# Attention and FFN block on one core: the whole score stack loaded at a unit's start, four weight sums on VectorE, residual stores and one activation load at other places of SyncE's queue

## The chip, the cores and the metric

The kernel runs on one core of a Trainium2 chip. The metric is the device time of one execution in microseconds (us); a lower time is better. The five engines are TensorE (PE, with its weight loads shown as PEld), VectorE (DVE), ScalarE (ACT), GpSimd (POOL) and SyncE (SP). Each works through its own list of instructions in order, and semaphores hold an instruction until what it needs is done. SyncE computes nothing here: it issues DMA transfers. ScalarE issues some transfers too, between its computations, and an issue that has to wait holds the ScalarE instructions behind it.

## The reference

One transformer block on x of 2048 tokens by 576, all in float32. `silu(c) @ w_mod` gives six vectors: shift, scale and gate for attention (sa, ca, ga) and for the FFN (sb, cb, gb).

```python
h = _layernorm(x) * (1 + ca) + sa
x = x + ga * _A_ref(h, wq, wk, wv, wo, beta)
h = _layernorm(x) * (1 + cb) + sb
x = x + gb * ((_silu(h @ w_gate) * (h @ w_up)) @ w_down)
```

`_A_ref` has 32 heads of 18 columns and works on four segments of 512 tokens. Inside a segment it is a softmax attention with a mask of -1e9; to it, weighted by a gate per head, comes a memory read-out `phi(q) M / (phi(q) z)`, where M and z are sums over the segments before. The FFN is 576 to 4608 and back.

## The kernel before

**Number format.** Float32 values are split into a high and a low part (tiles ending in h and l, or "hi" and "lo" rows), and a product is made of three matmuls: high by high, high by low, low by high. The high part is a ScalarE or GpSimd copy, the low part a VectorE subtraction.

**Stages.** First (0 to 255 us) the projections to q, k and v of the four segments, written to DRAM in a layout for attention (kD, qD, vD). Then attention in 32 units of four heads of one segment, with the output projection and layer norm of earlier segments interleaved (255 to 618). Then the output projection of the last segment (618 to 643), together with the preparation of the FFN's first operands. Then the FFN (643 to the end), for two halves t of 1024 tokens and 18 pairs p of 256 hidden columns. The order of all instructions after the projections is written out by hand (a manual schedule): the program's order is the order on each engine.

**A unit of attention.** Unit u works on a "stack" of k rows (`kst`, 108 rows by 2 by 512) and q rows (`qst`, 110 rows by 4 by 512). The 108 rows are two halves e=0 and e=1 of 54; each half is one DMA for k and one for q (L164, L165; 216 KB each). There are four buffers, and `load_unit(u + 3, e)` in unit u fills the one that unit u-1 has used. A unit has eleven steps k. At each step three things advance: `p2_step` (L588 on), which makes the transposed scores of unit u with TensorE (L599) and their exponentials with ScalarE (L602); `p1_seq`, which makes the scores of unit u+2 (L182) and takes row maxima with VectorE (L187); and the events that the table PAT names. The maxima are transposed, copied by ScalarE (L205, event "n", at step 4 or 2) and written by two small DMAs (L170, 8 KB each) into rows 108 and 109 of `qst`, where matmul L599 of the next unit subtracts them. SyncE's order in a unit is: half e=0 at step 0, the two maxima rows at step 4 (or 2), half e=1 at step 5, then v (L664, in units that load the next segment's v), besides loads of qf, wo, x and stores placed by events.

**The output projection of segment 3** (L1401 to L1425): for each of four token tiles i and two halves h there are 14 matmuls (`wo_m`, L729) into one of two PSUM banks, and VectorE adds the bank to the residual x (`wo_x`, L734, "xr"). The next but one half needs that bank back. In between stand, by the lists SS, HH and WW, eight sums of FFN weight blocks (`sum_o`, L1157, four for each of the two O tiles of the first pair, z=0 and z=1), splits of FFN activations (`y_here`) and splits of FFN weights (`prep_w`, L1166 and L1167). ScalarE stores the finished residual tiles 0 to 2 (L1410), each in the middle of the next tile, and SyncE the last one (L1426).

**The FFN** makes each 2 by 2 block product with seven products m instead of eight, from sums of weight blocks (tile O, seven slots) and sums of activation blocks (tile y, seven operands o). The activation operands 0, 1, 5 and 3 of the first token half are loaded by SyncE (`load_y`, L1122 and L1123, 1024 and 192 KB each), the others are made on the core. The first pair multiplies in the order m = 1, 6, 2, 7, 5, 4; product 5 is the first that reads operand 3. At its start SyncE loads the first rows of w_down (`load_d`, L1174), ScalarE stores the weight sums for the second token half (L1141), and SyncE loads the next pair's weights (L1135) after those stores have landed, as there are two O tiles.

Of the kernel before, what the change touches and what calls it, by code (L numbers as in the profile page):

```python
# [67 lines left out]
def f32(ap):  # L68
    return ap.bitcast(F32)
# [3 lines left out]
def block(ctx: ExitStack, tc: tile.TileContext, x, wqk, wv, wo, beta, wgu, wd, c, w_mod, out):  # L73
    nc = tc.nc
    def pool(stk, name, bufs=1, **kw):
        return stk.enter_context(tc.tile_pool(name=name, bufs=bufs, reuse_waits="tile", **kw))
# [5 lines left out]
    def chain(*g):  # L82
        for a in g:
            yield from a

    def run(g):
        for _ in g:
            pass
# [26 lines left out]
    NB = 4  # L115
# [29 lines left out]
    xD = [dr.tile([P, 4, D], F32, tag=f"xD{s}", name=f"xD{s}") for s in range(NSEG)]  # L145
# [9 lines left out]
    NU = len(units)  # L155
    mcol, pmt, mrow = {}, {}, {}

    def load_stack(u, b, es=(0, 1)):
        s, q = units[u]
        for e in es:  # L160
            v = [d[s].rearrange("f z t -> (f z) t").rearrange("(Q a e r) t -> Q e r a t", Q=8, a=2, e=2)[q, e]
                 for d in (kD, qD)]
            r = slice(54 * e, 54 * e + 54)
            nc.sync.dma_start(f32(kst[b][r]), v[0])  # L164
            nc.sync.dma_start(f32(qst[b][r, e:4:2, :]), v[1])  # L165
# [408 lines left out]
    opl_ = pool(p2, "op2")  # L574
    ps = pool(p2, "ps2", 2, space=PSUM)

    def load_unit(u, e):
        if u < NU:
            load_stack(u, u % NB, (e,))

    def p1_seq(u):
        if NE <= u < NU:
            for i in range(4):
                yield from p1_step(u, u % NB, 3 - i, ps, wk, 4)
# [3 lines left out]
    def p2_step(u, j):  # L588
        if u >= NU:
            return  # L590
        n = L - 128 * j
        per = L // n if n <= 256 else 1
        pt = pp_.tile([P, 4, n], F32, tag=f"P{j}", name="Pt", bufs=1)
        Pt[u, j] = pt
        for h in range(0, 4, per):
            bank = ps.tile([P, L], F32, tag="s2", name="s2", bufs=S2B)
            for g in range(h, h + per, 2):
                w = min(per, 2)
                nc.tensor.matmul(bank[:, n * (g - h):n * (g - h + w)].rearrange("p (a b) -> p a b", a=w),  # L599
                                 lhsT=kst[u % NB][0:110, g // 2, 128 * j:128 * j + 128],  # L600
                                 rhs=qst[u % NB][0:110, g:g + w, 128 * j:L], start=True, stop=True)
            nc.scalar.activation(pt[:, h:h + per, :n], bank[:, :n * per].rearrange("p (a b) -> p a b", a=per),  # L602
                                 AF.Exp, scale=SCALE)
            if h + per < 4:
                yield
        nc.gpsimd.affine_select(out=pt[:, :, :P], in_=pt[:, :, :P], pattern=[[0, 4], [1, P]], compare_op=ALU.is_ge,
                                fill=0.0, base=0, channel_multiplier=-1)
        yield
# [52 lines left out]
    def load_v(s, j):  # L661
        if j == 0:
            vq[s] = vp.tile([P, 4, VC], F32, tag="vq", name=f"vq{s}")
        nc.sync.dma_start(vq[s][:, j, :], vD[s][:, j, :])  # L664
# [5 lines left out]
    op = pool(p2r, "op", side="right")  # L670
# [22 lines left out]
    def load_xr(s, i):  # L693
        xr = o3.tile([P, D], F32, tag="xr", name="xr") if s < 3 or i in (0, 3) else xp.tile([P, D], F32, tag="xs", name="xr")
        r = L * s + P * i
        nc.sync.dma_start(xr, x[r:r + P, :])
        return xr
# [10 lines left out]
    def wo_s(s, i):  # L708
        nc.scalar.copy(oT[s, i][0], pto[s, i])

    def wo_t(s, i):
        oh, ol, _ = oT[s, i]
        nc.vector.tensor_tensor(ol, pto.pop((s, i)), f32(oh), op=ALU.subtract)
# [17 lines left out]
    def wo_x(s, i, h):  # L731
        xr = oT[s, i][2]
        sl = slice(288 * h, 288 * h + 288)
        nc.vector.tensor_tensor(xr[:, sl], wps[0][:, :288], xr[:, sl], op=ALU.add)  # L734
        if h == 1 and s < 3:
            (nc.scalar if (s, i) == (2, 3) else nc.sync).dma_start(xD[s][:, i, :], xr)

    lnv = {}
# [235 lines left out]
    def stage_a():  # L974
        sc = flat(yh12[:, 1])
        xb = [sc[:, L * i:L * i + L].rearrange("p (a b) -> p a b", b=P) for i in range(2)]
        mb = mbd[:, 0:2].rearrange("p a b c -> p (a b c)")
        st = [v.rearrange("p (a b) -> p a b", b=256).bitcast(F32R) for v in (sc[:, 2 * L:3 * L], mb[:, :L], mb[:, L:2 * L], gaB[:, :L])]
        pts = {}
        for i in range(6):  # L980
            kb, kh = divmod(i, 2)
            u = 18 + i
            n = P if kb < 2 else 96
            h = yh(kh, kb)
            at(11 * (u - 1) + 1 if i else 11 * u, lambda i=i, kh=kh, kb=kb: load_cols(xb[i % 2], 0, 0, kh, kb))
            g = step_of(u) if i else 11 * u + 10
            at(g, lambda i=i, n=n: trans4(xb[i % 2], n, pts, i))
            at(g + 1, lambda i=i, h=h, kh=kh, kb=kb: scaled(h, flat(pts.pop(i)), kh, kb))
            for hv in range(2):
                y_part(g + 2 + 3 * hv, kh, kb, h[:, 256 * hv:256 * hv + 256], lambda j=2 * i + hv: st[j % 4], hv)  # L990
# [130 lines left out]
    def load_y(t, o):  # L1121
        nc.sync.dma_start(f32(y[:, o, 0:4]), yD[t][o][:, 0:4])  # L1122
        nc.sync.dma_start(f32(y[0:96, o, 4]), yD[t][o][0:96, 4])  # L1123
# [4 lines left out]
    def flush():  # L1128
        while later:
            later.pop(0)()  # L1130
# [20 lines left out]
        nc.scalar.copy(r[0:96, c], o[0:96, c, 2, :])  # L1151
        later.append(lambda: nc.vector.tensor_tensor(r[32:64, c], o[32:64, c, 2, :], f32(r[32:64, c]), op=ALU.subtract))

    def sum_o(p, z, j):
        o = O[p, z]
        d, a, b, op = ((4, 3, 2, ALU.add), (5, 4, 0, ALU.subtract), (3, 0, 3, ALU.subtract), (6, 1, 5, ALU.subtract))[j]
        nc.gpsimd.tensor_tensor(o[:, d], o[:, a], o[:, b], op=op)  # L1157

    def store_r(p, z):
        nc.scalar.dma_start(rD[p][z], f32(R[z][0:96]))  # L1160
# [9 lines left out]
    def load_d(t, p):  # L1170
        RW[p] = r = rp.tile([P, 7, 288], F32, tag="d", name="dr_")
        if t == 0:
            for f in range(2):
                nc.sync.dma_start(r[:, 2 * f:2 * f + 2].rearrange("p a b -> p (a b)"), wd[2 * p + f])  # L1174
        else:
            nc.sync.dma_start(r[:, :NS[p]], wdD[p][:, :NS[p]])
# [165 lines left out]
    with tc.manual_schedule():  # L1342
# [4 lines left out]
        event("f", -1)  # L1347
        for u in range(NU + 1):
            s, q = divmod(u, 8)
            load_unit(u + 3, 0)  # L1350
            ga = chain(*[p2_step(u, j) for j in range(4)])
            gb = p1_seq(u + 2)
            for k in range(11):
                next(ga, None)
                next(gb, None)
                if u == 17 and k == 0:
                    stage_a()
                if u == 24 and k == 0:
                    stage_b()
                for ev in PAT[q // 4 * 2 + u % 2][k].split():  # L1360
                    event(ev, u)
                for f in sched.pop(11 * u + k, ()):
                    f()
                if k == 5:
                    load_unit(u + 3, 1)
                    if 3 <= q < 7 and s < 3:
                        load_v(s + 1, q - 3)
            run(ga)
            run(gb)
        p2.close()  # L1370
# [9 lines left out]
        xr3 = {i: load_xr(3, i) for i in range(3)}  # L1380
# [7 lines left out]
        load_y(0, 1)  # L1388
        xr3[3] = load_xr(3, 3)
        load_y(0, 5)  # L1390
        load_y(0, 3)
        wo_r(3, 0)
        wo_z(3)
        wo_r(3, 1)
# [6 lines left out]
        for i in range(4):  # L1401
            for h in range(2):
                for c in range(WC):
                    n = 8 * i + 4 * h + c
                    wo_m(3, i, h, c, 2)
                    if c == 3:
                        wo_x(3, i, h)
                    flush()
                    if i > 0 and h == 0 and c == 1:
                        nc.scalar.dma_start(xD[3][:, i - 1, :], xr3[i - 1])  # L1410
                    if n in SS:
                        j = SS.index(n)
                        sum_o(0, j // 4, j % 4)
                    if n in HH:
                        y_here(HH.index(n))
                    if n in WW:
                        j = WW.index(n)
                        if j < 2:
                            prep_r(0, 0, 0, j)
                        prep_w(0, 0, next(gw))  # L1420
                if h == 1 and i < 2:
                    wo_r(3, i + 2)
                    wo_s(3, i + 2)
                    wo_t(3, i + 2)
        flush()  # L1425
        nc.sync.dma_start(xD[3][:, 3, :], xr3[3])  # L1426
        p2r.close()
        p5.close()
        accp = pool(p4, "acc")
# [4 lines left out]
        p6 = ExitStack()  # L1434
        new_acc(accp, (2, 3, 4, 5))
        load_d(0, 0)
        seq = [(p, z, m) for t in range(2) for p in range(NPR) for z in range(2) for m in MP]
        late = {}
        prev = None
# [6 lines left out]
        for t in range(2):  # L1446
            for p in range(NPR):
# [16 lines left out]
                for k in range(14):  # L1464
                    z, m = ZM[k]
# [93 lines left out]
                    if is_plain(t, p):  # L1559
                        if k in DK[dl // 2]:  # L1560
                            j = DK[dl // 2].index(k)
# [74 lines left out]
```

## Time and profile before

| what | us |
|---|---|
| median of 3 executions | 1909.57 |
| lowest and highest | 1909.08, 1915.14 |
| the profiled execution, its own time | 1911.3 |
| its span on the core | 1909.4 |
| TensorE busy in the span | 1872.0 |
| VectorE, ScalarE, GpSimd busy | 1507.0, 933.7, 584.5 |

The profile is of one execution. A line of it gives an engine, a source line (L599), the tile written and those read, and the time; "[0.63 <-DMA qs<-qD]" behind a line means that the engine stood idle for 0.63 us before this instruction, and that the last thing which released it was that transfer. An engine with a q (SPq, ACTq) issues a DMA: the duration is that of the issue, not of the transfer. In views by stretch of time the last two columns are the mean busy share of the core's 16 DMA engines and the rate at which they moved data. TensorE's granted clock was 1.00 in all the stretches shown, 0.93 in the first 50 us.

### The profile page before, as it was taken

To read this page: it belongs to the slowest core of one execution; us is meant where nothing else is said; L and a number is where in the kernel's file an instruction comes from. 1 tells how busy PE (TensorE), PEld (TensorE's weight loads), DVE (VectorE), ACT (ScalarE), POOL (GpSimd) and SP (SyncE) were. 2 spreads that over 40 slices of the span, in tenths; PEclk is the share of its full clock that TensorE was granted. 3 is DMA by queue.
4 is the path that set the end of the run, shared out by engine and by line. 5 is a ranking of instruction groups with operands and counts; after the bars stand their busy time and mean duration, and the time that the engine had idled before them with its cause. 6 is when DMAs were issued, how large, how long until landed. Compare 5 with 4: busy or idle time off the path is not lost.

```text
span 1909.4 us, 30712 instructions
## 1 busy us (share of the span) xinstructions
PE 1872.0 (98%) x10927; PEld 1560.4 (82%) x10927; DVE 1507.0 (79%) x3273; ACT 933.7 (49%) x2060; POOL 584.5 (31%) x787
## 2 busy tenths in 40 slices
PE   7999999999999899999999999999999999999999
PEld 4888866676766788888888888888888888888888
DVE  6566358878886888888888888866888888888887
ACT  1222267768767543454454454444445454454542
POOL 5212236555556645435445435400000000000000
PEclk9999999999999999999999999999999999999999
DMA  6767555445654854454454554477333333333331
GB/s 199 258 220 255 197 177 152 132 138 155 195 157 129 311 199 154 161 196 143 162 192 141 183 164 129 153 263 231 102 124 102 95 105 101 123 102 101 108 105 59
DMA packets 179424, 304.31 MB, mean 159 GB/s; under 512 B 26152, under 2 KB 107688, under 8 KB 177352
## 3 DMA queue, kind: packets, MB, share of 16 engines
q1 hardware_dynamic: 150264, 244.40, 40.9%
q10 hardware_dynamic: 29008, 57.96, 8.6%
q8 instruction: 86, 1.41, 0.3%
q14 instruction: 66, 0.54, 0.1%
HBM read 187.98 MB, written 113.77 MB: 158 GB/s over the span
## 4 chain that ended last, share of the span: by engine, by line
PE 88%; DMA 3%; DVE 3%; ACT 2%; POOL 1%; issue 1%; SPq 1%; ACTq 0%; DVEq 0%; POOLq 0%
PE A L1202 23%; PE pd L1323 13%; PE C L1202 11%; PE pd L1306 9%; PE B L1202 6%; PE pp L99 5%; PE s L599 4%; PE av L619 3%; PE s L182 3%; PE pv L99 3%; PE pw L729 2%; DMA qs<-qD 1%; DMA y<-yD 1%; PE pn L800 1%; ACT Pt L602 1%
## 5 line engine op out<-in xcount | busy, mean ns | idle before, releaser
L1202 PE MATMUL A<-y,wh 128*128 128x512 f32 x1152 | 406.1, 393 | 3.4 <-ACT B L1248 1.0
L187 DVE CUSTOM_DVE_ANT_0 junk<-s,tri 128x256 bf16<-128x256 f32 (+3 forms) x512 | 228.8, 487 | 71.9 <-PE s L182 64.4
L1167 DVE TENSOR_TENSOR wl<-O,wh 128x256 fp32r<-128x256 f32 x504 | 260.3, 521 | 2.8 <-ACT wh L1166 2.3
L1202 PEld LDWEIGHTS A<-y,wh 128*128 128x128 f32 x1152 | 216.6, 188 | 47.6 <-ACT B L1248 1.5
L1202 PE MATMUL A<-y,wl 128*128 128x512 f32 x576 | 226.7, 394 | 0.0
L602 ACT ACTIVATE Pt<-s 128x512 f32<-128x512 f32 (+1 forms) x352 | 188.0, 559 | 75.2 <-PE s L599 70.9
L1157 POOL TENSOR_TENSOR O<-O 128x384 f32<-128x384 f32 x144 | 164.6, 1156 | 169.2 <-DMA O<-in_wgu_dram 65.0
L1311 DVE TENSOR_TENSOR acc<-acc,pd 128x576 f32<-128x576 f32 x216 | 162.4, 752 | 58.6 <-PE pd L1306 52.0
L1202 PE MATMUL C<-y,wh 128*128 128x512 f32 x576 | 202.6, 392 | 1.6 <-DVE cu L1225 1.6
L1166 ACT CAST wh<-O 128x256 fp32r<-128x256 f32 x504 | 196.9, 405 | 7.6 <-DVE wl L1167 3.5
L1323 PE MATMUL pd<-dh,al 128*128 128x288 f32 x640 | 189.1, 296 | 0.0
L1323 PE MATMUL pd<-dh,ah 128*128 128x288 f32 x640 | 189.1, 295 | 0.0
L1323 PE MATMUL pd<-dl,ah 128*128 128x288 f32 x640 | 188.9, 295 | 0.0
L1327 DVE TENSOR_TENSOR acc<-acc,pd 128x576 f32<-128x576 f32 x156 | 116.9, 750 | 90.4 <-PE pd L1323 90.0
L1266 ACT CAST ah<-sg 128x512 fp32r<-128x512 f32 x192 | 119.2, 621 | 84.0 <-DVE sg L1226 77.9
L599 PE MATMUL s<-qs,ks 110*128 110x512 f32 (+2 forms) x384 | 150.1, 407 | 2.1 <-ACT Pt L602 2.0
L182 PE MATMUL s<-ks,qs 108*128 108x256 f32 (+3 forms) x512 | 141.1, 328 | 5.9 <-DVE mx L187 3.6
L1267 DVE TENSOR_TENSOR al<-sg,ah 128x512 fp32r<-128x512 f32 x192 | 135.8, 707 | 8.8 <-ACT ah L1266 8.5
L1306 PE MATMUL pd<-dh,ah 128*128 128x288 f32 x448 | 133.0, 297 | 0.0
L1306 PE MATMUL pd<-dh,al 128*128 128x288 f32 x448 | 132.5, 296 | 0.0
L1306 PE MATMUL pd<-dl,ah 128*128 128x288 f32 x448 | 132.3, 295 | 0.0
L1202 PEld LDWEIGHTS C<-y,wh 128*128 128x128 f32 x576 | 108.3, 188 | 22.2 <-DVE cu L1225 2.1
(360 smaller groups left out, 4405.4 us busy)
## 6 DMA issues: line engine op xcount, KB each, us to landing
O<-in_wgu_dram SPq DMA_DIRECT2D x36, 768.0 KB
oD<-O ACTq DMA_DIRECT2D x36, 512.0 KB
O<-oD SPq DMA_DIRECT2D x36, 512.0 KB
ks<-kD SPq DMA_DIRECT2D x64, 216.0 KB
qs<-qD SPq DMA_DIRECT2D x64, 216.0 KB
O<-in_wgu_dram SPq DMA_DIRECT2D x36, 384.0 KB
rD<-wr ACTq DMA_DIRECT2D x36, 336.0 KB
wr<-rD SPq DMA_DIRECT2D x35, 336.0 KB
```

Source lines behind the costliest of these rows:

```text
L99: nc.tensor.matmul(ps, lhsT=a, rhs=b, start=(k == 0), stop=(k == 13))
L182: nc.tensor.matmul(bank[:, n * (h - h0):n * (h - h0) + n], lhsT=qst[b][0:108, h, 128 * i:128 * i + 128], rhs=kst[b][0:108, h // 2, 0:n], s ...
L187: nc.vector.tensor_tensor_reduce(junk[:, :n], bank[:, n * (h - h0):n * (h - h0) + n], tri[:, L - n:], 1.0, -3e38, op0=ALU.add, op1=ALU.max ...
L599: nc.tensor.matmul(bank[:, n * (g - h):n * (g - h + w)].rearrange("p (a b) -> p a b", a=w), lhsT=kst[u % NB][0:110, g // 2, 128 * j:128 * ...
L602: nc.scalar.activation(pt[:, h:h + per, :n], bank[:, :n * per].rearrange("p (a b) -> p a b", a=per), AF.Exp, scale=SCALE)
L1157: nc.gpsimd.tensor_tensor(o[:, d], o[:, a], o[:, b], op=op)
L1166: nc.scalar.copy(wh, o)
L1167: later.append(lambda: nc.vector.tensor_tensor(wl, o, f32(wh), op=ALU.subtract))
L1202: nc.tensor.matmul(bank, lhsT=a, rhs=b, start=(first and n == 0), stop=(n == 6), skip_group_check=not first)
L1306: nc.tensor.matmul(pd[:, i, :288], lhsT=a[:, tk], rhs=w, start=(k == 0), stop=(k == 2))
L1311: nc.vector.tensor_tensor(o, o, pd[:, :, :288], op=ALU.add)
L1323: nc.tensor.matmul(pd[:, i, :288], lhsT=a[:, tk], rhs=w, start=(k == 0), stop=(k == 5))
```

## The change

Four things change; the computation stays the same.

- Both halves of a stack are loaded at step 0 of a unit. The maxima rows and v follow them on SyncE's queue.
- Of the eight weight sums in the last output projection, the four of z=1 are done by VectorE instead of GpSimd, at the same places of the written order.
- The residual tiles of segment 3 are all stored by SyncE, each right behind its last addition, as in the other segments.
- Operand 3 of the first half's activations is loaded behind the first w_down load, after the output projection, and no longer ahead of it.

```diff
-    def load_stack(u, b, es=(0, 1)):
+    def load_stack(u, b):
         s, q = units[u]
-        for e in es:
+        for e in range(2):
...
-    def load_unit(u, e):
+    def load_unit(u):
         if u < NU:
-            load_stack(u, u % NB, (e,))
+            load_stack(u, u % NB)
...
         nc.vector.tensor_tensor(xr[:, sl], wps[0][:, :288], xr[:, sl], op=ALU.add)
-        if h == 1 and s < 3:
+        if h == 1:
             (nc.scalar if (s, i) == (2, 3) else nc.sync).dma_start(xD[s][:, i, :], xr)
...
-    def sum_o(p, z, j):
+    def sum_o(p, z, j, eng=nc.gpsimd):
         o = O[p, z]
...
-        nc.gpsimd.tensor_tensor(o[:, d], o[:, a], o[:, b], op=op)
+        eng.tensor_tensor(o[:, d], o[:, a], o[:, b], op=op)
...
-            load_unit(u + 3, 0)
+            load_unit(u + 3)
...
-                if k == 5:
-                    load_unit(u + 3, 1)
-                    if 3 <= q < 7 and s < 3:
-                        load_v(s + 1, q - 3)
+                if k == 5 and 3 <= q < 7 and s < 3:
+                    load_v(s + 1, q - 3)
...
         load_y(0, 5)
-        load_y(0, 3)
...
                     flush()
-                    if i > 0 and h == 0 and c == 1:
-                        nc.scalar.dma_start(xD[3][:, i - 1, :], xr3[i - 1])
                     if n in SS:
                         j = SS.index(n)
-                        sum_o(0, j // 4, j % 4)
+                        sum_o(0, j // 4, j % 4, nc.vector if j > 3 else nc.gpsimd)
...
         flush()
-        nc.sync.dma_start(xD[3][:, 3, :], xr3[3])
...
         load_d(0, 0)
+        load_y(0, 3)
```

## The prediction

> **What bounds the kernel now.** I read the page's busy shares first, then the busy time by stage, then who waited for whom on TensorE, then the order in time around each wait.
>
> ```profile
> PE 1872.0 (98%) x10927; PEld 1560.4 (82%) x10927; DVE 1507.0 (79%) x3273; ACT 933.7 (49%) x2060; POOL 584.5 (31%) x787
> ```
>
> 98% is an average. By stage (attention, output projection of the last segment, start of the FFN, rest of the FFN; the columns are length, then busy PE, PEld, DVE, ACT, POOL, clock, DMA share, GB/s):
>
> ```profile
> 255.00:618.00 363.00, 355.09 (x2585) 237.81 (x2584) 290.19 (x1176) 270.55 (x556) 200.82 (x382) 1.00 0.52 149
> 618.00:643.00 25.00, 20.91 (x166) 19.70 (x159) 18.35 (x29) 10.02 (x21) 14.90 (x13) 1.00 0.93 335
> 643.00:675.00 32.00, 27.73 (x117) 21.15 (x116) 28.27 (x39) 18.43 (x42) 16.54 (x14) 1.00 0.81 274
> 675.00:1880.00 1205.00, 1203.97 (x6567) 1058.45 (x6566) 1015.16 (x1708) 568.95 (x1320) 276.67 (x251) 1.00 0.44 143
> ```
>
> From 675 on TensorE idles 1.0 us in 1205: nothing the diff touches can change that part, which only starts sooner or later. The diff edits the first three rows, where TensorE idles 7.9, 4.1 and 4.3 us. Two of its waits there belong to lines that the change moves (total, times, longest):
>
> ```profile
> PE pw L729 <- DVE xr L734: 3.4, 2, 1.8
> PE s L182 <- DMA qs<-qD: 2.2, 5, 1.0
> ```
>
> **Part 1, the stack load.** One unit in the order of time on SyncE's queue, the matmul that then waited, and the DMA share in between:
>
> ```profile
> 263.56 0.29 SPq L164 DMA_DIRECT2D ks<-kD  x1
> 263.89 0.35 SPq L165 DMA_DIRECT2D qs<-qD  x1
> 269.11 1.21 SPq L170 DMA_DIRECT2D qs<-mr  x2
> 270.36 0.49 SPq L164 DMA_DIRECT2D ks<-kD  x1
> 270.90 0.34 SPq L165 DMA_DIRECT2D qs<-qD  x1
> ...
> 275.72 0.47 PE L182 MATMUL s<-ks,qs 108*128 108x512 f32 x1 [0.63 <-DMA qs<-qD]
> ...
> 264.00:267.50 3.50, 3.50 (x32) 1.44 (x27) 2.45 (x13) 1.85 (x5) 3.08 (x6) 1.00 0.47 129
> 267.50:270.00 2.50, 2.33 (x13) 1.64 (x13) 2.25 (x9) 2.47 (x7) 0.64 (x1) 1.00 0.00 0
> ```
>
> The second half (e=1) stands behind the two maxima rows (L170), which wait for ScalarE's copy, and lands 4.8 us after its issue, at the first score matmul of the next unit. Issued at step 0 it goes out 6 us sooner, at about 264.3, and has the idle 267.5 to 270 to itself. All five waits (0.63, 0.17, 0.98, 0.15, 0.22) go: at most -2.15. The same loop of ScalarE and VectorE stands behind them (57 weight loads in this stage wait for the exponentials, 31.7 us), so some may come back as that wait; least gain 0. I take -2.0, since in each case PE was the engine that waited.
>
> What it adds: L170 now has 442 KB more ahead of it on SyncE's ring. A pair takes 3.2 us (264.3 to 267.45 in slices of half a microsecond). From the end of the second L170 issue to the next unit's first exponent-side matmul, which reads those rows, there are 3.85 us or more in every unit. Tightest is the one with L170 at 289.54: the first pair's data ends at 290.2 there, so the second would end by 293.4, and the rows are read at 294.54: 1.0 us spare; next 2.0. Cost 0; ends 0 and what rival C gives. v (L664), qf (L772) and wo (L904) keep their place after L170 or lose only the e=1 pair ahead of them; their users are a unit or more later.
>
> Whether the second pair really queues was bounded from 0 to 3.2 us, as the first pair fills only 0.58 to 0.63 of the 16 engines. [...]
>
> **Part 2, the output projection.** GpSimd's eight weight sums and VectorE at the same work with and without them:
>
> ```profile
> 625.89 10.38 POOL L1157 TENSOR_TENSOR O<-O 128x384 f32<-128x384 f32 x8
> ...
> 631.73 1.11 DVE L1167 TENSOR_TENSOR wl<-O,wh 128x256 fp32r<-128x256 f32 x1
> 637.10 0.41 DVE L1167 TENSOR_TENSOR wl<-O,wh 128x256 fp32r<-128x256 f32 x1
> ...
> 633.35 0.37 PE L729 MATMUL pw<-woh,oh 128*128 128x288 f32 x1 [1.55 <-DVE xr L734]
> 637.23 0.40 PE L729 MATMUL pw<-woh,oh 128*128 128x288 f32 x1 [1.80 <-DVE xr L734]
> ```
>
> While GpSimd sums, a VectorE instruction with both inputs in SBUF takes 1.1 to 1.5 us instead of 0.41 to 0.69. That backlog delays the residual add (xr), which frees the bank that TensorE waits for. With four sums left, GpSimd ends at 625.89 + 4 x 1.30 = 631.1. VectorE's rows from there at their short durations: wr ends 631.35, wl 631.8, xr 632.25 (was 633.21); wr 632.95, wl 633.35, y 634.1, xr 634.55 (was 637.18). TensorE's halves (1.9 us each) then start at 632.3, 634.6, 636.85, 638.75 and the last ends at 640.65, not 643.02: -2.4. The four sums on VectorE cost 0.55 each (between 0.41 for 256 and 0.68 for 512 columns), 2.2 us; one stands ahead of an add, three ahead of the last, at 639.75 to 641.4. No later half waits for the last add, and the first FFN bank doesn't either, so they cost TensorE 0; without that cover 1.2. Ends: -3.4 (both waits gone) and 0.
>
> The three residual stores leave ScalarE, which stood 3.50 and 2.51 us at them; it was not what TensorE waited for. On SyncE they wait for the adds in the order in which they come. Behind the last stand down's first load (L1174) and now y's operand 3: the last store would issue at 641.9 (was 643.71), L1174 at 642.4 and 642.8 (was 644.22), the y load at 643.3.
>
> **Part 3, the moved y load.** It was issued at 634.61, the small part at 642.68 (SyncE stood 7.7 us there, until a residual store had landed; now the store of the third tile, out by 639, is the one it waits for, and hides). It is read by the fifth product, at 650.45; with part 2 at about 648.05. What it now meets:
>
> ```profile
> 650.45 0.40 PE L1202 MATMUL C<-y,wh 128*128 128x512 f32 x1
> ...
> 616.00:640.00 24.00, 19.53 (x155) 17.24 (x155) 16.98 (x26) 9.87 (x20) 16.74 (x16) 1.00 0.99 350
> 640.00:644.00 4.00, 4.00 (x29) 3.82 (x29) 2.15 (x7) 1.24 (x3) 0.00 (x0) 1.00 0.44 154
> 644.00:650.00 6.00, 5.33 (x24) 4.02 (x23) 3.88 (x6) 4.39 (x10) 2.33 (x2) 1.00 0.96 312
> 650.00:659.00 9.00, 8.07 (x35) 6.33 (x34) 8.84 (x11) 5.91 (x13) 6.87 (x7) 1.00 0.93 316
> ```
>
> It leaves a stretch that ends idle (0.44) and joins one that is full until 659. Ahead of it on its queue are the last store (0.29 MB) and L1174 (0.59), beside it ScalarE's two weight stores (1.05 MB); itself it is 1.25 MB. From 642 at 310 to 350 GB/s it lands at 648.8 if ScalarE's queue gets nothing, 652.5 if the two share evenly. I take 650.9, between them: TensorE waits 2.8 us at the fifth product, which starts 0.45 later than before. Some comes back at once: the 0.93 us that the next product waited at 653.16 is for a copy behind VectorE, now ahead; from there it is 0.5 early. Then the second pair's weights: their first load (L1135, 649.98) waits for the weight store to land and stands behind y, so it gains nothing; the second was issued at 659.61, on VectorE's last weight split, about as early or late as TensorE. So the dense part starts 0.5 sooner. Ends: 2.9 sooner (y hidden), 2 later (even sharing and the weights behind it late by the rest of 1.25 MB / 0.34 = 3.7 us less 1.7).
>
> [...]
>
> **Sum.** -2.0 in attention and -0.5 at the start of the FFN: -2.5. The profiled execution took 1911.3 (span 1909.4 and 1.9 around it), so 1908.8; it is 1.7 above the median, 1909.57, against which the forecast is 1907.1.
>
> **Rivals.**
> A, the forecast: 1905.5 to 1908.5, 0.45.
> B, y lands in time and the gain of part 2 stays: -2.0 - 2.4 to -2.0 - 2.9, 1904.9; 0.22. For it: 640 to 644 is nearly idle. Against: 644 to 659 is full.
> C, slower: the maxima rows land behind the whole stack after they are needed. Price: beyond the spare, every microsecond of queueing costs one in each tight unit. It decides once a pair takes 1.1 us more than 3.2 in the tightest units; six units have 4.5 us or less after the issue; at 1 us each the forecast plus 6 is 1913.1, and at 1 us in half of the 28 units plus 14, 1921; above the time before from plus 2.5 on. For it: both pairs are alike and serial. Against: the 1.0 us is the worst case, and 3.85 us the least. 0.13.
> D, VectorE's slow rows don't come back or y lands after 653: no gain in part 2, +2 at the FFN: 1909.57 - 2.0 + 2 to + 4, 1909.6 to 1911.6; 0.20. For it: the sums are added to the engine that made TensorE wait.
>
> The time is that of A. The range reaches from B's better end to most of D and the start of C: 1903 to 1913. A measurement of this kernel can tell about 0.3% (5.7 us) from no change; Faster needs the far ends together (-2.15, -3.4 and some of the third row's 4.3 us of idle): 0.08, out of B. Slower is C's worse half, with 0.03 out of D: 0.1. Within: 0.82.
>
> **What would show it.** Right: no wait of L182's matmul for qs; the wl rows between 631 and 637 at 0.41; TensorE's first FFN product at about 640.7 less 2; then a wait of the fifth product for y of 2 to 3 us. Wrong: a wait of L599's matmuls for qs<-mr (C); no wait for y (B); the first add rows still late, or the stage from 675 on shorter or longer than 1234.

## The result, and the profile after

The changed kernel takes 1908.87 us (median of 20 runs, 1902.93 to 1915.08), the kernel before, beside it, 1913.87 (20 runs, 1909.08 to 1918.15). The ratio is 0.9977 with a 95% interval from 0.9969 to 0.9986: 4.4 us faster, between 2.7 and 5.9. That is a change of 0.2%, inside the 0.3% of the forecast, and more than its 2.5 us. Ratios here and below are of executions in the faster of two states, which leaves out one execution of e8 (3659.63 us).

All stages in the tables below are cut at the same instructions of TensorE: the first exponent-side matmul (L599) of unit 0, that of unit 31, the first FFN product (L1202), and the first matmul of the down projection. Each row is one profiled execution (us).

| | ahead of attention | attention | output projection | start of the FFN | rest | span |
|---|---|---|---|---|---|---|
| before | 254.96 | 354.10 | 33.96 | 34.67 | 1231.71 | 1909.4 |
| after | 256.81 | 349.68 | 31.42 | 37.65 | 1231.14 | 1906.7 |
| difference | +1.85 | -4.42 | -2.54 | +2.98 | -0.57 | -2.7 |

The first column holds no changed code; in twelve traces of kernels whose code there is the same it lies between 254.96 and 258.99. The profile of the kernel after by stages (length, then busy PE, PEld, DVE, ACT, POOL, clock, DMA share, GB/s), and the eight microseconds around the fifth FFN product:

```profile
255.00:609.00 354.00, 348.77 (x2552) 236.07 (x2551) 287.34 (x1172) 265.84 (x548) 197.44 (x376) 1.00 0.53 152
609.00:638.00 29.00, 27.02 (x214) 23.48 (x207) 18.52 (x37) 14.85 (x31) 13.46 (x15) 1.00 0.78 276
638.00:675.50 37.50, 31.57 (x127) 24.44 (x126) 29.52 (x45) 21.37 (x47) 16.68 (x14) 0.95 0.79 267
675.50:1880.00 1204.50, 1203.83 (x6570) 1058.41 (x6570) 1018.30 (x1705) 567.98 (x1317) 276.57 (x251) 1.00 0.44 143
...
647.00:651.00 4.00, 3.12 (x8) 2.46 (x9) 1.04 (x3) 0.86 (x3) 2.36 (x3) 0.68 1.06 373
651.00:655.00 4.00, 4.00 (x17) 3.23 (x16) 3.11 (x6) 2.23 (x5) 1.28 (x2) 0.89 1.01 347
```

The third row is the only one with a clock below 1.00 (0.95), and the last two say where: between 647 and 655. TensorE idles 5.2 us in attention here (7.9 in the row of before, which is 9 us longer), 2.0 in the second row (was 4.1) and 5.9 in the third (was 4.3).

The order in time of the changed kernel: the stack on SyncE's queue, the two new waits of TensorE, the last output projection on VectorE, and the FFN's fifth and sixth product:

```profile
265.41 0.29 SPq L164 DMA_DIRECT2D ks<-kD  x1
265.74 0.34 SPq L165 DMA_DIRECT2D qs<-qD  x1
266.13 0.34 SPq L164 DMA_DIRECT2D ks<-kD  x1
266.51 0.34 SPq L165 DMA_DIRECT2D qs<-qD  x1
270.94 1.21 SPq L170 DMA_DIRECT2D qs<-mr  x2
...
296.80 0.47 PE L599 MATMUL s<-qs,ks 110*128 110x512 f32 x1 [1.22 <-DMA qs<-mr]
...
475.22 0.40 PE L182 MATMUL s<-ks,qs 108*128 108x512 f32 x1
475.46 0.40 PE L599 MATMUL s<-qs,ks 110*128 110x512 f32 x1
475.69 0.40 PE L182 MATMUL s<-ks,qs 108*128 108x512 f32 x1
...
629.14 0.43 DVE L1167 TENSOR_TENSOR wl<-O,wh 128x256 fp32r<-128x256 f32 x1
...
631.03 0.69 DVE L1046 TENSOR_TENSOR y<-yh,y 128x512 fp32r<-128x512 f32 x1
...
647.88 0.50 PE L1202 MATMUL C<-y,wh 128*128 128x512 f32 x1 [2.39 <-DMA y<-yD]
...
649.73 0.63 PE L1202 MATMUL C<-y,wh 128*128 128x512 f32 x1
650.16 0.63 PE L1202 MATMUL C<-y,wr 96*128 96x512 f32 x1
```

No L182 matmul waits for qs any more. One L599 matmul now waits for the maxima rows (296.80). VectorE's wl rows take 0.43 us. The fifth FFN product waits 2.39 us for operand 3, and behind that wait a matmul of 512 columns takes 0.63 us instead of 0.40.

### The profile page after: what moved, and what is told of

Same layout as the page of the kernel before. It is cut to its first block, busy times and chain, and to the rows that moved or that the text cites. A ratio compares the mean times of both kernels' runs of the same rounds, so it can differ in the third digit from the quotient of the medians.

```text
span 1906.7 us, 30703 instructions
## 1 busy us (share of the span) xinstructions
PE 1870.6 (98%) x10927; PEld 1560.4 (82%) x10927; DVE 1507.7 (79%) x3277; ACT 933.8 (49%) x2060; POOL 579.1 (30%) x783
## 4 chain that ended last, share of the span: by engine, by line
PE 91%; DVE 3%; ACT 2%; DMA 2%; POOL 1%; issue 1%; SPq 0%; ACTq 0%; POOLq 0%; DVEq 0%
PE A L1202 23%; PE pd L1323 13%; PE C L1202 12%; PE pd L1306 9%; PE B L1202 6%; PE pp L99 5%; PE s L599 4%; PE av L619 4%; PE s L182 4%; PE pv L99 3%; PE pw L729 3%; PE pn L800 1%; ACT Pt L602 1%; PE px L640 1%; PE pm L448 1%
## 5 line engine op out<-in xcount | busy, mean ns | idle before, releaser
L1202 PE MATMUL A<-y,wh 128*128 128x512 f32 x1152 | 406.3, 393 | 3.1 <-ACT B L1248 2.5
L1202 PEld LDWEIGHTS A<-y,wh 128*128 128x128 f32 x1152 | 217.1, 188 | 47.0 <-ACT B L1248 3.2
L1202 PE MATMUL A<-y,wl 128*128 128x512 f32 x576 | 226.9, 394 | 0.0
L1157 POOL TENSOR_TENSOR O<-O 128x384 f32<-128x384 f32 x140 | 159.4, 1151 | 175.9 <-DMA O<-in_wgu_dram 73.8
L1202 PE MATMUL C<-y,wh 128*128 128x512 f32 x576 | 203.3, 394 | 2.8 <-DMA y<-yD 2.4
L599 PE MATMUL s<-qs,ks 110*128 110x512 f32 (+2 forms) x384 | 150.0, 407 | 3.7 <-ACT Pt L602 2.4
L182 PE MATMUL s<-ks,qs 108*128 108x256 f32 (+3 forms) x512 | 140.3, 326 | 3.2 <-DVE mx L187 3.1
L1202 PEld LDWEIGHTS C<-y,wh 128*128 128x128 f32 x576 | 108.5, 188 | 23.8 <-DMA y<-yD 2.8
```

Source lines behind the costliest of these rows:

```text
L182: nc.tensor.matmul(bank[:, n * (h - h0):n * (h - h0) + n], lhsT=qst[b][0:108, h, 128 * i:128 * i + 128], rhs=kst[b][0:108, h // 2, 0:n], s ...
L1157: eng.tensor_tensor(o[:, d], o[:, a], o[:, b], op=op)
L1202: nc.tensor.matmul(bank, lhsT=a, rhs=b, start=(first and n == 0), stop=(n == 6), skip_group_check=not first)
```

## The experiments

Stages of each, as above (e5, e6, e11, e12: one execution; the others a profile and timed runs). "Against before" is the ratio with its 95% interval.

| | ahead | attention | projection | FFN start | rest | against before |
|---|---|---|---|---|---|---|
| e1 stack alone | 256.01 | 349.33 | 33.93 | 34.75 | 1230.78 | 0.9956 (0.9944 to 0.9968) |
| e2 sums alone | 255.55 | 354.82 | 31.44 | 35.51 | 1232.98 | 0.9988 (0.9979 to 0.9997) |
| e3 y later alone | 258.76 | 357.55 | 33.95 | 38.64 | 1233.5 | 1.0016 (1.0007 to 1.0026) |
| e4 after, y back | 256.23 | 349.81 | 31.45 | 35.31 | 1232.9 | 0.9960 (0.9948 to 0.9972) |
| e5 after, wait filled | 258.99 | 349.64 | 31.44 | 36.71 | 1231.52 | |
| e6 after, half loaded twice | 256.34 | 377.84 | 31.41 | 37.22 | 1231.99 | |
| e7 after, 48 + 6 rows | 262.66 | 348.74 | 31.43 | 36.69 | 1232.18 | 0.9999 (0.9989 to 1.0009) |
| e8 e4 with 48 + 6 rows | 258.77 | 349.08 | 31.43 | 35.39 | 1231.03 | 0.9984 (0.9974 to 0.9995) |
| e9 e4, 48 + 6 in attention | 255.64 | 348.96 | 31.44 | 35.73 | 1233.53 | 0.9960 (0.9948 to 0.9973) |
| e10 after, 48 + 6 in attention | 258.72 | 349.04 | 31.45 | 37.73 | 1233.36 | 0.9962 (0.9948 to 0.9975) |
| e11 before again | 258.59 | 355.74 | 35.36 | 34.15 | 1232.86 | |
| e12 before, third | 256.32 | 356.44 | 33.94 | 35.21 | 1231.99 | |

**e1, the stack alone.** The kernel before, with the second half moved to step 0.

```diff
             load_unit(u + 3, 0)
+            load_unit(u + 3, 1)
...
                 if k == 5:
-                    load_unit(u + 3, 1)
```

> Part 1 alone on the kernel before. Theory (the late half of the stack cost more than the waits on it, 4.4 us in the changed kernel's attention stage against 2.15 us of waits): attention, from the first L599 matmul of unit 0 to that of unit 31, takes 349.7 (it was 354.1), no L182 matmul waits for qs, one L599 matmul waits 1.2 us for the maxima rows near 296; the stages from 618 on as before; time 4.4 us below before. Rival (the extra 2.2 us are the spread of that stage between executions, seen in waits for VectorE's maxima): attention takes 351.5 to 352.5, time 2 below.

Attention 349.33, so the whole gain of attention is this part's. The waits for the maxima rows were two short ones (0.35 and 0.25 us) instead of one of 1.2. The whole time fell by 8.4 us (6.1 to 10.7), almost twice what was expected; e11 and e12 look for the rest.

**e2, the four sums alone.**

```diff
-                        sum_o(0, j // 4, j % 4)
+                        sum_o(0, j // 4, j % 4, nc.vector if j > 3 else nc.gpsimd)
```

> The four weight sums on VectorE alone. Theory (GpSimd's sums slowed VectorE's two-input rows, and that backlog held TensorE): from unit 31's first L599 matmul to the first FFN product 31.4 us (it was 34.0), the wl rows in that stage at 0.41; the FFN's start keeps it, since y's operand is loaded early, so time 2 to 2.5 below before. Rival (the stores leaving ScalarE made the difference): 33.5 to 34 us in that stretch and the time of before.

The one wait for xr that TensorE has left in the last projection (there were two, 1.55 and 1.80 us), and VectorE's rows, in the order of time:

```profile
633.04 0.43 DVE L1167 TENSOR_TENSOR wl<-O,wh 128x256 fp32r<-128x256 f32 x1
...
633.98 0.37 PE L729 MATMUL pw<-woh,oh 128*128 128x288 f32 x1 [0.86 <-DVE xr L734]
...
639.32 0.55 DVE L1157 TENSOR_TENSOR O<-O 128x384 f32<-128x384 f32 x1
```

The projection takes 31.44 as in the changed kernel, with the stores still on ScalarE: the stores' move is worth nothing there, the sums are worth all. 0.8 us of it are given back at the FFN's start (35.51), where a product now waits 3.27 us for one of VectorE's additions (L1225) and the clock is 0.50 for 3.4 us behind it; the whole time is 2.3 us less (0.6 to 4.0).

**e3, the y load alone.**

```diff
-        load_y(0, 3)
         wo_r(3, 0)
...
         load_d(0, 0)
+        load_y(0, 3)
```

> Only y's operand 3 loaded behind w_down's first load. Theory (the fifth product waits for it, and the clock granted falls after the wait): the wait is 2 to 4 us, the fifth and sixth products take 2.9 and 2.2 us at a clock of 0.7 instead of 1.6; from the first FFN product to TensorE's last restart 32 to 34 us (it was 29.7); time 2.5 to 4 above before. Rival (the wait is absorbed by the waits that follow, the weights' load and GpSimd's sums): 29.7 to 30.5 us and the time of before.

The fifth product waits 2.91 us for y and the clock is 0.62 between 660 and 664; +3.1 us (1.3 to 5.0). The last wait ahead of the dense part came at 30.5 us and not at 32 to 34, but the down projection starts after 38.64 us, the longest FFN start of all.

**e4, the changed kernel with the y load back at its old place.**

```diff
         load_y(0, 5)
+        load_y(0, 3)
...
         load_d(0, 0)
-        load_y(0, 3)
```

> The changed kernel with y's operand 3 loaded at its old place. Theory: no wait for y, clock 1.0 throughout, 29.7 us or less from the first FFN product to TensorE's last restart (32.7 in the changed kernel); time 2.5 to 3 below the changed kernel, 7 below before. Rival (the load ahead of the residual stores holds SyncE's queue, or the later waits come to the same end): 31.5 to 33 us there and the changed kernel's time within 1 us.

No wait for y, clock 1.00, and 7.7 us below before (5.4 to 10.0), 3.3 more than the changed kernel's gain, as expected. The last restart (TensorE's last start behind a wait ahead of the dense part, here one of 0.26 us) comes at 30.3 us and not at 29.7 or less.

**e5, the wait filled.** Does the clock fall because TensorE stands idle?

```diff
+                    if dl and k == 5:
+                        pf = ps.tile([P, 2, L], F32, tag="dn", name="pf", bufs=2)
+                        for _ in range(12):
+                            nc.tensor.matmul(pf[:, 0], lhsT=W[0, 5][0][:, 0], rhs=y[:, 0, 0], start=True, stop=True)
```

> The changed kernel with twelve more matmuls of 512 columns, whose result nothing reads, ahead of the fifth FFN product of the first token half; the output is as before. Theory (TensorE's clock falls because TensorE stood idle for 2.4 us): the filled wait leaves no idle stretch over 1 us there, the granted clock stays at 1.00 from 648 on and the fifth and sixth product take 1.6 us each instead of 2.90 and 2.18; from the first FFN product to the last restart ahead of the dense part 31 us instead of 32.7. Rival (the clock falls for another reason, such as the start of a stretch of dense work or the DMA load): the clock is below 0.9 between 648 and 652 again and the two products take 5 us.

Its windows over the same stretch of the FFN (it starts 2.2 us later here):

```profile
647.00:651.00 4.00, 4.00 (x19) 3.29 (x18) 3.90 (x5) 2.73 (x6) 3.84 (x4) 1.00 1.02 346
651.00:655.00 4.00, 4.00 (x19) 3.30 (x18) 2.95 (x7) 2.11 (x5) 0.09 (x1) 1.00 1.04 294
```

With the same load beside it and no idle time, the clock stays at 1.00 (0.68 and 0.89 in the changed kernel's rows) and the products take 1.6 us each: here it is the idle time that lowers the clock. Of the 1.9 us that the slow products had cost, the FFN's start keeps 0.9 (36.71 instead of 37.65); two waits behind it, 1.97 and 1.07 us, take the rest, and the last restart comes at 31.7 us, not at 31.

**e6, half a stack loaded twice.** Another pair of loads ahead of the maxima rows.

```diff
             load_unit(u + 3)
+            if u + 3 < NU:
+                load_stack(u + 3, (u + 3) % NB, (1,))
```

> The changed kernel with half e=1 of each stack loaded a second time right behind the first (the same data again). Theory (the whole stack stands ahead of the maxima rows on the same DMA engines, and these rows had only 1 to 2 us to spare in the tight units): another 3.2 us ahead of them makes the exponent-side matmul wait for the maxima rows in at least six units, up to 4.4 us in the one that now waits 1.2; attention 349.7 plus 6 to 14, 356 to 364 us. Rival (the one wait of 1.2 us comes from a late copy on ScalarE or from other loads, and the queueing has no part in it): at most two such waits, attention 349 to 352.

Its waits in attention, and its windows around the longest of them:

```profile
PE s L599 <- DMA qs<-mr: 19.9, 14, 3.2
```

```profile
314.00:316.00 2.00, 1.43 (x8) 0.88 (x12) 0.68 (x3) 0.92 (x2) 0.00 (x0) 0.93 0.75 240
316.00:318.00 2.00, 2.00 (x12) 1.11 (x5) 0.64 (x5) 0.61 (x2) 0.00 (x0) 0.50 0.56 144
318.00:320.00 2.00, 2.00 (x15) 1.03 (x15) 1.63 (x6) 1.10 (x4) 0.89 (x3) 0.72 0.56 187
```

Fourteen waits, 19.9 us, for the maxima rows: rival C's mechanism exists and its place was named rightly. Attention grew by 28 us, not by 6 to 14: more than twice as many units as counted on were tight (none by more than 3.2 us), and four stretches at half clock lie behind waits of 1.69 to 3.20 us (8.5 us by their clock).

**e7, rows 48 and 6.** Each transfer of 54 rows in two.

```diff
+            for c0, c1 in ((0, 48), (48, 54)):
+                r = slice(54 * e + c0, 54 * e + c1)
-            nc.sync.dma_start(f32(kst[b][r]), v[0])
-            nc.sync.dma_start(f32(qst[b][r, e:4:2, :]), v[1])
+                nc.sync.dma_start(f32(kst[b][r]), v[0][c0:c1])
+                nc.sync.dma_start(f32(qst[b][r, e:4:2, :]), v[1][c0:c1])
```

> The changed kernel with each transfer of 54 rows cut into one of 48 and one of 6. Theory (a transfer of 54 rows uses 9 of the 16 DMA engines, so that the two halves of a stack stand behind each other on these nine): the DMA share while a stack loads goes from 0.6 to 0.85 or more, the stack is in 1.5 us sooner, the wait of 1.2 us for the maxima rows is gone, attention 348.3 to 348.8; whole time 1 us less than the changed kernel. Rival (the share of 0.6 comes from the length of the runs or from the queue, not from the row count): share 0.6 and attention 349.7 as before, or longer by the eight issues instead of four, which take SyncE 1.4 us more in each unit.

Attention 348.74 and one wait of 0.2 us for the rows, as expected; but the whole time is that of the kernel before, since the stage ahead of attention took 262.66 us, 5.9 more than in the trace of the changed kernel and 3.7 more than in the longest of the other traces. Three waits of TensorE between 100 and 263 us, at two lines, that no trace with 54-row loads there shows:

```profile
PE pv L99 <- ACT pf L466: 2.2, 1, 2.2
PE pt L236 <- DVE x L231: 1.6, 2, 1.3
```

Behind them the clock is 0.50 for 3.4 us (from 185.1). The first three stacks are loaded in that stage, by the same function, on the same queue.

**e8, the same with the y load at its old place.** The edits of e4 and e7 together.

> The cut of e7 together with the y load at its old place (as in e4): the whole stack at step 0 in transfers of 48 and 6 rows, four sums on VectorE, the stores on SyncE. Theory (each part pays at its own place): attention 348.5, output projection 31.4, first FFN product to the last restart at most 30, whole time 8 us below the kernel before, 1 us below e4. Rival (what is won ahead of the FFN is lost at its start): output projection and FFN start together as long as in e4, and no gain beyond it.

Attention 349.08 and projection 31.43, near the 348.5 and 31.4 expected; the last restart comes at 30.4 us and not at 30 at most. The whole time is 3.1 us below before instead of 8, and the same waits (1.7 and 1.6 us) stand ahead of attention.

**e9 and e10, rows 48 and 6 in attention only.**

```diff
-    def load_stack(u, b):
+    def load_stack(u, b, cuts=((0, 54),)):
...
-            load_stack(u, u % NB)
+            load_stack(u, u % NB, ((0, 48), (48, 54)))
```

> As e8, but the transfers are cut into 48 and 6 rows only for the stacks loaded during attention (units 3 to 31); the three stacks loaded in the projections keep 54 rows. Theory (e7 and e8 lost in the projections what they won in attention, since their first stacks took twice the issues on SyncE ahead of loads that the projections wait for): the projection stage is as in e4 (first exponent-side matmul at 256 to 257 us), attention 348.7 to 349.1, output projection 31.4; whole time 0.5 to 1 us below e4, ratio to before about 0.995. Rival (the doubled issues cost in attention or later, in a way that the profile of e8 does not show): ratio to before 0.998 or more, as e8.

> The changed kernel, with the stacks of attention alone (units 3 to 31) in transfers of 48 and 6 rows. Theory: attention 348.7 instead of 349.7, everything else as in the changed kernel; whole time 1 us less, ratio to before about 0.997. If the wait of the fifth FFN product for the y load lasts over 2 us again, TensorE's clock falls to half for 3.4 us behind it, which costs 1.7 us. Rival: as e7, ratio 1.000.

The windows of e9 from one microsecond after the first load of a unit's stack (264.2) on:

```profile
265.20:266.20 1.00, 1.00 (x10) 0.46 (x10) 0.48 (x5) 0.28 (x1) 0.92 (x3) 1.00 0.85 203
266.20:267.20 1.00, 1.00 (x11) 0.55 (x4) 0.60 (x2) 0.42 (x2) 0.91 (x3) 1.00 1.04 197
267.20:268.20 1.00, 1.00 (x13) 0.44 (x12) 0.86 (x3) 1.00 (x3) 0.72 (x1) 1.00 1.02 191
268.20:269.20 1.00, 0.94 (x5) 0.54 (x4) 0.81 (x3) 1.00 (x3) 0.00 (x0) 1.00 0.93 217
269.20:270.20 1.00, 0.88 (x4) 0.62 (x5) 0.94 (x5) 0.97 (x4) 0.64 (x1) 1.00 0.31 78
```

And those of the changed kernel at the same place, where the loads begin at 265.4:

```profile
266.40:267.40 1.00, 1.00 (x13) 0.46 (x10) 0.49 (x5) 0.32 (x1) 0.92 (x3) 1.00 0.45 123
267.40:268.40 1.00, 1.00 (x11) 0.60 (x4) 0.55 (x2) 0.43 (x2) 0.91 (x3) 1.00 0.61 190
268.40:269.40 1.00, 1.00 (x13) 0.44 (x12) 0.92 (x3) 1.00 (x3) 0.68 (x1) 1.00 0.61 162
269.40:270.40 1.00, 0.91 (x5) 0.49 (x3) 0.81 (x3) 1.00 (x3) 0.00 (x0) 1.00 0.57 201
270.40:271.40 1.00, 0.93 (x4) 0.67 (x5) 0.94 (x5) 0.97 (x5) 0.64 (x1) 1.00 0.58 178
```

The share rises from 0.6 to 1.0, the rate far less, and the stack is in about one microsecond sooner (5.3 us after its first issue instead of 6.2). The waits ahead of attention are gone again, and the ratio falls from 0.9984 (e8) to 0.9960 (e9) and from 0.9999 (e7) to 0.9962 (e10), so the doubled early loads were the cost in e7 and e8. Attention gains 0.6 to 0.9 us; in the whole time that cannot be told apart (e9 and e4 both 0.9960). e10 repeats the y wait (3.18 us) with the half clock behind it.

**e11 and e12, the kernel before again.**

> The kernel before, unchanged, for a second profiled execution of it. The medians of e1 stand 8.4 us below the kernel before and its trace only 4.8 us in attention. Theory (the stalls on the late half of a stack differ from one execution to the next, and the first profiled execution of the kernel before was a mild one, 2.6 us below its median): attention takes 354.8 to 357.6, as in the traces of e2 and e3, whose attention is the same. Rival (attention repeats and the rest lies elsewhere): attention 354.0 to 354.3.

> The kernel before once more, a third profiled execution. Theory and rival as for e11: attention between 354.8 and 357.6 by the one, at 354.0 to 354.3 by the other; in both the waits of the first-half score matmul for the late half stand in the same units as in the first profile.

Attention took 355.74 and 356.44. With e2 and e3, whose attention is the same code, the kernel before shows 354.10, 354.82, 355.74, 356.44 and 357.55, mean 355.7; the four traces with the whole stack at step 0 in 54 rows show 349.33 to 349.81, mean 349.6. So the execution that the forecast was worked from was the mildest of five, and the part is worth 6.1 us on average, at the edge of e1's interval. That the waits for the late half stand in the same units each time was not borne out: they are in units 2, 10, 20, 21 and 29 in the first profile, in 4, 10, 12 and 20 in e11, and in 4, 5, 10, 12, 18, 21 and 29 in e12. The projection's 35.36 in e11 holds 3.4 us at a clock of 0.50 (from 644.0, behind a wait of 1.78 us). In e11, and again in e12, two score matmuls, of units 4 and 12, wait openly for the late half:

```profile
300.42 0.47 PE L182 MATMUL s<-ks,qs 108*128 108x512 f32 x1 [1.18 <-DMA qs<-qD]
...
386.35 0.47 PE L182 MATMUL s<-ks,qs 108*128 108x512 f32 x1 [0.86 <-DMA qs<-qD]
```

## Why the prediction was right, and where by cancellation

The forecast of -2.5 us was made from -2.0 in attention and -0.5 at the FFN; the two profiled executions differ by -2.7. These 2.7 are made of -4.4 in attention, +0.4 from there to the dense part, -0.6 behind it, and 1.9 us ahead of attention that no edit made, so that the two numbers agree by luck. So do the times: 1907.1 lies near 1908.87 since its base, the median of 3 executions (1909.57), was 4.3 us below the median of 20 (1913.87), and the gain taken off it was some 2 us too small.

**Part 1** had the right mechanism and too small a size. "All five waits (0.63, 0.17, 0.98, 0.15, 0.22) go: at most -2.15" is the step that failed, for two reasons that the same trace of before shows:

```profile
295.12 0.40 PE L599 MATMUL s<-qs,ks 110*128 110x512 f32 x1
296.25 0.47 PE L182 MATMUL s<-ks,qs 108*128 108x512 f32 x1 [0.74 <-DVE mx L187]
...
475.29 0.50 PE L599 MATMUL s<-qs,ks 110*128 110x512 f32 x1
475.94 0.47 PE L182 MATMUL s<-ks,qs 108*128 108x512 f32 x1
476.25 0.39 PE L599 MATMUL s<-qs,ks 110*128 110x512 f32 x1
477.61 0.47 PE L182 MATMUL s<-ks,qs 108*128 108x512 f32 x1 [0.98 <-DMA qs<-qD]
```

First, a stall costs more than the idle time printed behind it. From the start of the L599 matmul at 476.25 to that of the next L182 are 1.36 us; in the changed kernel the same pair is 0.23 apart (475.46, 475.69). The loss is 1.13 us, and 0.98 is printed: running matmuls overlap (0.40 us each, starts 0.23 apart), and a stall ends that. The unit also has a smaller gap that is not printed, 0.65 us from 475.29 to the first L182 (0.33 in the changed kernel). Taken by the length of their units, the five listed waits cost 3.4 us (0.83, 0.43, 1.61, 0.43, 0.13), not 2.15.

Second, two waits of the very same matmul, 0.74 in unit 4 and 0.73 in unit 12, were put down to VectorE's maxima and so not counted; their units became 1.01 and 0.99 us shorter. In e11 the same two are put down to the transfer, and in every kernel with the early half they are gone. With 0.2 us in unit 18 that makes 5.6 us; the new wait for the maxima rows, 1.26 us by the unit's length, leaves 4.3 of the 4.4.

That wait is **rival C** in the one unit that the prediction called tightest, with "1.0 us spare": cost 0 was wrong by 1.2 us there and right in the others. The spare was counted to the end of the stack's data, with nothing for the rows' own transfer behind it: their last packet starts at 295.29, and the matmul, ready at 295.58, starts at 296.80. e6 shows that only the size kept C small. The pair does queue behind the first: the DMA share stays at 0.57 to 0.61 for four microseconds. Of 16 engines that is 9.1 to 9.8, beside the nine that the expectation of e7 counts on; in the trace of the changed kernel exactly nine of the load's 2 KB packets are under way for 59% of the time from 266.8 to 271.3, and 9.4 on average. In e9, with 48 and 6 rows, the share is 0.93 to 1.04 in the three microseconds that the load fills. Two readings of this part are slightly off and change nothing: the least time from the issue of the rows to their use is 3.79 us, in unit 2 (3.55 in unit 31, where no stack is loaded any more), not 3.85, and the weight loads that wait for the exponentials between 255 and 618 are 60 with 33.2 us, not 57 with 31.7.

**Part 2** came out as worked: -2.54 against -2.4, wl at 0.43, the sums at 0.55 and free for TensorE. Beside GpSimd's sums the rows of before with both inputs in SBUF had taken 0.79 to 1.48 us (the prediction has 1.1 to 1.5), wl 1.11 and 1.13. One stall of 0.9 us is left, the other is gone.

**Part 3** had the wait right (2.39 against 2.8 us) and its consequence wrong. "So the dense part starts 0.5 sooner" failed: the FFN's start became 2.98 us longer and took back all of part 2's gain, and by these two stages the dense part starts 0.4 later. The fifth and sixth product took 2.90 and 2.18 us instead of 1.6 each, 1.9 us that no term held, as TensorE's clock falls behind the wait (0.50 for 3.41 us); e5 shows the cause, e4 that this fall goes with the load (in e6 the wait, 2.29 us, has none behind it). By e5 only 0.9 of the 1.9 us reach the end of the stage. The rest of the loss is the wait itself, of which less came back than the prediction took. The profile's chain through this stage runs from y's transfer (until 647.84) over the two slow products (until 652.97) to VectorE's weight split, the second pair's weight load, GpSimd's sums and the last restart. The prediction had that load follow VectorE's split, which was right, so it inherits the delay: it is issued 18.2 us after the first FFN product, before 16.6. The last restart then came 32.7 us after the first FFN product instead of 29.7.

**Rival B** (y in time) did not come: y landed 9.92 us after the first FFN product, which on the prediction's scale is 650.6, beside the 650.9 taken from rates. In all six traces with the late load the product waits, but for e5, where the filling covers it. **Rival D** did not come either: VectorE's rows did turn short; but its loss at the FFN came all the same, by the wait and the clock (2.98 us, not 2).

The time lies within the forecast's range, and the change is below the 0.3% that the forecast took a measurement to tell, which had 0.82 of the chance; twenty executions of each kernel tell it all the same (0.9969 to 0.9986). Rival A, the forecast itself, came in kind (a gain in attention, a wait for y, no gain left of part 2), but its band, 1905.5 to 1908.5 or 4.1 to 1.1 us below its base, misses both 1908.87 and 4.4. That the result rests on the y load's loss set against the larger gain in attention is the part to learn from.

Without the y load's move the sum is better: e1, e4 and e9 stand at 0.9956 to 0.9960, and their intervals do not tell them apart. The lowest median, 1905.61, is e9's. How much the move costs in the whole time is less clear. Alone it costs 3.1 us (e3), and e4 against the changed kernel says 3.3, though the intervals of those two overlap a little; but e10 has the move, and an FFN start of 37.73, and stands at 0.9962 beside e9's 0.9960, five executions each. Nor do the gains of e1 and e2 add up: e4 holds both parts and is not below e1.

Open: why the late half comes at other times in other executions, why e2, e4, e8 and e9 give back 0.6 to 1.1 us of the sums' gain at the FFN's start (the waits there change place, and behind those of e2 and e8 the clock falls, but not in e4 and e9; a cause was only seen, not tried), and what e1 gains beyond the 6.1 us of attention, if anything.

## What to carry to other kernels

Price a stall from start to start against the same pair of instructions without it, and count every wait of that instruction at that place, whatever releaser the profile names. Where a change makes TensorE wait some two microseconds or more, price a fall of the clock too: here it came behind 13 of 18 such waits, with 1.7 us of TensorE's work lost each time. A gain ahead of a stage that starts with loads is only there if that stage does not turn it into a wait; look at the next stage's first reads before adding the two.

## What the runs showed of the hardware that was not expected

Fourteen traces show 40 waits of TensorE of 1.2 us or more between the start of attention and the first down product. Behind all 6 of 2.79 us and more the granted clock fell to 0.50, behind 7 of 12 from 1.97 to 2.47 us, and behind 3 of 22 from 1.20 to 1.80 us. The traces' record of the granted clock shows why equal waits end differently: in each of the fourteen it changes only at whole multiples of 3.413 us from its first entry, so in these traces it goes by a fixed grid of windows. Here are two waits of the changed kernel on that grid, 2.39 us up to 647.88 and 2.47 us up to 670.61:

```profile
645.02:648.43 3.41, 1.02 (x5) 0.53 (x4) 2.88 (x3) 2.83 (x6) 3.33 (x4) 1.00 0.99 339
648.43:651.84 3.41, 3.41 (x9) 2.63 (x8) 0.95 (x2) 0.22 (x1) 1.01 (x2) 0.50 1.08 362
...
665.50:668.91 3.41, 2.25 (x9) 1.24 (x7) 3.38 (x6) 0.00 (x0) 2.38 (x2) 1.00 0.00 1
668.91:672.32 3.41, 1.71 (x7) 1.43 (x8) 2.39 (x5) 2.57 (x6) 0.00 (x0) 1.00 1.00 378
672.32:675.74 3.42, 3.42 (x17) 2.81 (x16) 3.05 (x7) 2.82 (x6) 0.00 (x0) 1.00 0.46 119
```

The first wait lies in one window, with 2.39 us of idle time in it, and the next window runs at 0.50. The second is spread over two, with 1.16 and 1.70 us, and no window falls. The wait of 2.29 us in e6 is spread too (0.94 and 1.35). In the fourteen traces between the start of attention and the first down product, all 13 windows with 1.97 us or more of idle time are followed by one at 0.50, and 3 of 23 with 1.3 to 1.8 us. With less than 1.3 us none is, apart from the window at half clock in which e6's longer fall goes on. Each fall takes one window, 3.41 us at half speed or 1.7 us of work; only one of them (e6, after 1.69 us) lasted two.

Falls of this kind are not the late y load's alone: in e1, e2, e8 and e12, which load y early, one follows another wait at the FFN's start, of 1.97 to 3.27 us.

Cutting 54 rows into 48 and 6 fills the DMA engines to 1.0 and brings the stack in only 0.9 us of 6.2 sooner: a higher DMA share (0.93 to 1.04 against 0.57 to 0.61) was not a rate higher by as much (191 to 217 GB/s against 162 to 201).
